# Packed attention and SwiGLU on one core: the sign of the float64 weights goes through a Prelu in the first pass of their conversion

## The chip, the cores and the metric

The kernel runs on one core of a Trainium2 chip. The metric is the device time of one execution in microseconds. A core has five engines with queues of their own: PE (TensorE, matrix products), DVE (VectorE), ACT (ScalarE), POOL (GpSimd) and SP (SyncE, which here issues the DMAs). Each takes the instructions of its queue in order and waits by semaphores for the others. All of them work on SBUF (128 partitions); products of PE land in PSUM.

## The reference

For 8 batches of 8 heads, 32 packed queries `p` attend to 576 keys and values, and then the 576 queries `q` attend to the 32 packed results. The heads are put side by side to 4608 tokens of 512 numbers, which pass an RMS norm and a SwiGLU layer:

```python
def _attn_ref(q, k, v, p):          # sm_attn: softmax attention, scale 1/sqrt(64)
    p_packed = sm_attn(p, k, v)
    out = sm_attn(q, p_packed, p_packed)
    return out.astype(np.float32)

def _moe_ref(x, w_gate, w_val, w_out, rms_g):
    rms = np.sqrt(np.mean(x * x, axis=-1, keepdims=True) + 1e-06)
    xn = x / rms * rms_g
    g = xn @ w_gate
    silu = g * (1.0 / (1.0 + np.exp(-g)))
    val = xn @ w_val
    return (silu * val @ w_out).astype(np.float32)
```

`q`, `k`, `v`, `p` and `rms_g` come as float32. The three weight matrices (512 x 1536, 512 x 1536, 1536 x 512) come as float64, and the kernel reads each number as two 32-bit words, a low one and a high one. The high word has the sign, 11 bits of exponent and the 20 upper bits of the mantissa.

## The kernel before, in words

The 4608 tokens are 12 units of 384 (`u`), a unit is 3 query tiles of 128 tokens. Products that have to be more exact than one half-precision product are made of three, with each operand split into a high and a low float16 part (`split`, L127: ACT writes the high part, L129, DVE the low part, L130).

The work before the steady loop is a prologue, whose order is written by hand in the string `PROLOGUE` (L24). Each letter advances a generator by one step: `s` is the packed attention of batch 0 (`stage1_gen`), `0 1 2` are the first three query tiles (`qtile_gen`), `u` the norm of unit 0 (`unit_gen`), `w` the weights (`weights_gen`), `p` the product of the packed results with the gate and value weights (`pw_gen`, `pw_chunk`, L471) and `a` the gate and value products of unit 0 (`moe_ft`, L667, with Silu in L674). After it, the loop over units runs 24 slots a unit, in which the next batches' attention and the next units' query tiles are laid between the products (`moe_ft`, then `moe_out` with the products `po`, L688). Tile's planner then puts the instructions of each engine into an order of its own by estimated costs, so that a queue's order is not everywhere that of the program.

`weights_gen` loads the weights in 18 chunks of 1 MB, each 128 partitions of 1024 float64 numbers. Chunks 1 to 12 are `w_gate` and `w_val` in turn (`load_gv`, two for each of six column blocks `c`), and the last six are `w_out` (`load_wo`). SP issues each load (L180, L206) into a raw buffer. The first twelve go round over five such buffers: three lie in the memory of `wo32`, which is not yet in use, and two are `wst` buffers; the last six share the two `wst` buffers. `to_f32` (L153) makes float32 of a chunk:

- L158: ACT reads the high words as if they were float32, takes the absolute value and multiplies by 2^-111 (`HI_SCALE`). The factor sets the exponent right for what follows.
- L159: DVE shifts the bits left by 3.
- L160: DVE ors the top three bits of the low words in.
- The sign, which Abs took away, is put back in one of two ways, by the letter in `SGW` (for the twelve) or `SGO` (for the six). With "D", DVE takes the sign bit of the high word and ors it in (L167). With "P", ACT writes the sign as 1 or -1 to a bfloat16 tile `sg` (L164), and POOL multiplies (L165). `sg` has the tag "o", of which there are two buffers; `sq` and later `o` use the same.

The letters alternate, so nine chunks have their sign put back by DVE and nine by ACT and POOL. After `to_f32` of a gate or value chunk, ACT squares the result to bfloat16 (`sq`, L187), PE sums the squares over the rows (L189), and DVE works out powers of two as scales from the largest sum (L194, `norm_scale`: L114, L118, L119, and L198); POOL multiplies them to `gv_sc` and `wo_sc` (L199 to L201). After a `w_out` chunk DVE takes the maxima (L211). When all six are there, `wo_scale` makes the scale (L218 to L227), and `wo_split` (L229) splits `w_out` in place, in six steps on ACT, DVE and POOL (L232 to L237); only then do the products `po` have their weights.

Between these, the prologue's query tiles run chains of small steps over PE, DVE, ACT and POOL: `rest_q` with the scores `ps` (L549), the maximum (L563), Exp (L566), the sum (L568), the reciprocal (L571), the normalisation (L572), the transposes (L610), the values `px` (L589) and their squares (L595), and POOL's norm (L597 to L602). `unit_gen` takes the norms of the three tiles together (L617, L619), and POOL multiplies the scales of the weights by the result (L658, L632).

Of the kernel before, what the change touches and what calls it, by code (L numbers as in the profile page):

```python
# [9 lines left out]
F32 = mybir.dt.float32  # L10
F16 = mybir.dt.float16
BF16 = mybir.dt.bfloat16
U32 = mybir.dt.uint32
AF = mybir.ActivationFunctionType
ALU = mybir.AluOpType
AX = mybir.AxisListType

P = 128
EXP_MASK = 0x7F800000

SGW = "PDPDPDPDPDPD"
SGO = "DPDPDP"
WOS = "ADADDA"
PROLOGUE = "s w " + "s " * 13 + "0 1 2 " * 5 + "u " * 4 + "w " * 18 + "p a a w " * 6 + "w " * 6  # L24

# [1 line left out]
HI_SCALE = 2.0**-111  # L27
# [3 lines left out]
def tile_packed_attention_then_swiglu(  # L31
# [27 lines left out]
    nc = tc.nc  # L59
# [17 lines left out]
    pool = ctx.enter_context(tc.tile_pool(name="pool", bufs=2))  # L77
# [22 lines left out]
    wo32 = cpool.tile([P, NFT, DM], F32, name="wo32")  # L100
# [11 lines left out]
    def norm_scale(u, s, sums):  # L112

        nc.vector.tensor_scalar(  # L114
            u.bitcast(U32), sums.bitcast(U32), 24, 23,
            ALU.logical_shift_right, ALU.logical_shift_left,
        )
        nc.vector.tensor_scalar(u, u, 2.0**-126, 2.0**51, ALU.max, ALU.mult)  # L118
        nc.vector.tensor_single_scalar(s.bitcast(U32), u.bitcast(U32), EXP_MASK, ALU.bitwise_xor)  # L119
# [30 lines left out]
    wctx = ExitStack()  # L150
    wpool = wctx.enter_context(tc.tile_pool(name="wpool", bufs=2))

    def to_f32(dst, st, pool_signs):  # L153


        lo, hi = st[..., 0], st[..., 1]
        d = dst.bitcast(U32)
        nc.scalar.activation(dst, hi.bitcast(F32), AF.Abs, scale=HI_SCALE)  # L158
        nc.vector.tensor_single_scalar(d, d, 3, ALU.logical_shift_left)  # L159
        nc.vector.scalar_tensor_tensor(d, lo, 29, d, ALU.logical_shift_right, ALU.bitwise_or)  # L160
        if pool_signs:
            sg = pool.tile([P, 1024], BF16, name="sg", tag="o", bufs=2)
            sg = sg.rearrange("p (a n) -> p a n", a=dst.shape[1])
            nc.scalar.activation(sg, hi.bitcast(F32), AF.Sign)  # L164
            nc.gpsimd.tensor_tensor(dst, dst, sg, ALU.mult)  # L165
        else:
            nc.vector.scalar_tensor_tensor(d, hi, 0x80000000, d, ALU.bitwise_and, ALU.bitwise_or)  # L167

    def load_gv(c):

        pn = ps_m.tile([P, 512], F32, name="pn", tag="pm")
        for n, w in enumerate((w_gate, w_val)):

            room = (2 * c + n) % 5
            if room < 3:
                raw = wo32[:, 4 * room : 4 * room + 4, :].bitcast(U32).rearrange("p a n -> p (a n)")
            else:
                raw = wpool.tile([P, 4 * DM], U32, name="wst", tag="wst", bufs=2)
            raw = raw.rearrange("p (k n e) -> p k n e", k=NKT, e=2)
            nc.sync.dma_start(  # L180
                raw.rearrange("p k n e -> p k (n e)"),
                w[:, 4 * c * P : 4 * (c + 1) * P].rearrange("(kt p) f -> p kt f", p=P),
            )
            x = wgv[:, c, :, n, :]
            to_f32(x, raw, SGW[2 * c + n] == "P")
            sq = pool.tile([P, NKT, 2 * P], BF16, name="sq", tag="o", bufs=2)
            nc.scalar.activation(sq, x, AF.Square)  # L187
            for kt in range(NKT):
                nc.tensor.matmul(  # L189
                    pn[:, 256 * n : 256 * n + 256], onesb, sq[:, kt, :], start=(kt == 0), stop=(kt == NKT - 1)  # L190
                )
            yield
        mx = wpool.tile([P, 2], F32, name="wmx", tag="w1", bufs=6)
        nc.vector.tensor_reduce(mx, pn.rearrange("p (w f) -> p w f", w=2), AX.X, ALU.max)  # L194
        u = wpool.tile([P, 2], F32, name="wu", tag="w1", bufs=6)
        s = wpool.tile([P, 2], F32, name="ws", tag="w1", bufs=6)
        norm_scale(u, s, mx)
        nc.vector.tensor_scalar_mul(pw_sc[:, c, :], s, 2.0**-15)  # L198
        nc.gpsimd.tensor_scalar(gv_sc[:, c, 0:1], u[:, 0:1], gmax, 2.0**-5, ALU.mult, ALU.mult)  # L199
        nc.gpsimd.tensor_scalar(gv_sc[:, c, 1:2], s[:, 0:1], gmax_r, 2.0**-12, ALU.mult, ALU.mult)  # L200
        nc.gpsimd.tensor_scalar(wo_sc[:, c : c + 1], u[:, 0:1], u[:, 1:2], gsq, ALU.mult, ALU.mult)  # L201

    def load_wo(i):

        raw = wpool.tile([P, 2, DM, 2], U32, name="wst", tag="wst", bufs=2)
        nc.sync.dma_start(  # L206
            raw.rearrange("p a n e -> p a (n e)"),
            w_out[2 * i * P : 2 * (i + 1) * P, :].rearrange("(a p) n -> p a n", p=P),
        )
        to_f32(wo32[:, 2 * i : 2 * i + 2, :], raw, SGO[i] == "P")  # L210
        nc.vector.tensor_reduce(  # L211
            wo_mx[:, 2 * i : 2 * i + 2], wo32[:, 2 * i : 2 * i + 2, :], AX.X, ALU.max, apply_absolute_value=True
        )
# [25 lines left out]
    def weights_gen():  # L239
        load_g()  # L240
        yield
        for c in range(NFC):
            yield from load_gv(c)
            yield
        for i in range(NFT // 2):
            load_wo(i)
            yield
        wo_scale()
        for i in range(NFT // 2):
            wo_split(i)  # L250
            yield
# [487 lines left out]
    for t in range(TPU, NU * TPU):  # L739
        u, i = divmod(t, TPU)  # L740
# [6 lines left out]
    for b in range(1, B):  # L747
        t = b * S // P
        u, i = divmod(t, TPU)
# [62 lines left out]
```

## Time and profile before

| | |
|---|---|
| median of three runs | 925.7 us (921.09 to 926.83) |
| the profiled execution | 921.36 us |
| its span | 919.6 us |
| mean granted clock of PE in it | 0.949 of full speed |
| busy PE, DVE, ACT, POOL | 771.5, 565.5, 563.8, 111.0 us |

The span is the time from the first to the last instruction in the profile; what is missing to the execution's own time (1.8 us) lies around it. Engines are busy side by side, so their busy times do not add up to the span. Busy shares over the whole span mix a prologue of some 170 us, in which PE is often idle, and the steady loop, in which PE is busy for most of the time. The chain of work that ended last starts at the last instruction and goes back, at each step to what released it, or to the instruction before it on its engine; it is given in order of time, as start, duration, engine, tile and line. A row of a line's instructions gives the minimum, median and maximum duration in ns. In a timeline, the bracket at the end says how long the engine was idle before the instruction and what released it.

### The profile page before, as it was taken

To read this page: it belongs to the slowest core of one execution; us is meant where nothing else is said; L and a number is where in the kernel's file an instruction comes from. 1 tells how busy PE (TensorE), PEld (TensorE's weight loads), DVE (VectorE), ACT (ScalarE), POOL (GpSimd) and SP (SyncE) were. 2 spreads that over 40 slices of the span, in tenths; PEclk is the share of its full clock that TensorE was granted. 3 is DMA by queue.
4 is the path that set the end of the run, shared out by engine and by line. 5 is a ranking of instruction groups with operands and counts; after the bars stand their busy time and mean duration, and the time that the engine had idled before them with its cause. 6 is when DMAs were issued, how large, how long until landed. Compare 5 with 4: busy or idle time off the path is not lost.

```text
span 919.6 us, 16693 instructions
## 1 busy us (share of the span) xinstructions
PE 771.5 (84%) x6392; PEld 435.4 (47%) x6392; DVE 565.5 (61%) x1406; ACT 563.8 (61%) x1074; POOL 111.0 (12%) x228
## 2 busy tenths in 40 slices
PE   4545866765889988898999988999999899989998
PEld 3332223324745544446745444557555345467453
DVE  4697796564755756846746657657647558466250
ACT  3465656545756758847756659657668479477240
POOL 2258111310000010010010000100000100100000
PEclk9856698996999999999999999999999999999999
DMA  9764327333083264224272282140751622221200
GB/s 248 252 201 146 100 84 153 83 81 64 7 181 92 52 145 93 43 58 81 56 178 64 52 195 55 39 100 7 139 132 32 135 53 53 58 65 24 57 1 35
DMA packets 174000, 84.98 MB, mean 92 GB/s; under 512 B 149216, under 2 KB 161504, under 8 KB 173920
## 3 DMA queue, kind: packets, MB, share of 16 engines
q1 hardware_dynamic: 173920, 83.91, 38.8%
q8 instruction: 50, 0.82, 0.4%
q14 instruction: 30, 0.25, 0.1%
HBM read 47.97 MB, written 9.44 MB: 62 GB/s over the span
## 4 chain that ended last, share of the span: by engine, by line
PE 41%; DVE 18%; ACT 17%; DMA 12%; issue 6%; POOL 3%; SPq 1%; ACTq 0%; DVEq 0%; POOLq 0%
PE po L688 14%; PE pg L667 8%; PE pv L667 7%; DMA aT<-ehl 5%; PE pp_w L471 4%; ACT t L674 3%; ACT L674 3%; PE px L589 2%; DVE t L675 2%; DVE pwt L130 2%; DMA kT<-khl 2%; DMA kf<-in_k_dram 2%; DVE h L678 1%; ACT pwt L129 1%; DMA aTu<-ahl 1%
## 5 line engine op out<-in xcount | busy, mean ns | idle before, releaser
L688 PE MATMUL po<-wo,h 128*128 128x512 f16 x1296 | 295.7, 383 | 3.8 <-ACT t L674 1.4
L667 PEld LDWEIGHTS <-pwt 128*128 128x128 f16 x2304 | 206.8, 99 | 155.5 <-issue 46.1
L667 PE MATMUL pg<-aTu,pwt 128*128 128x384 f16 (+1 forms) x1152 | 172.4, 292 | 42.0 <-ACT t L674 14.1
L688 PEld LDWEIGHTS <-h 128*128 128x128 f16 x1296 | 123.9, 99 | 156.5 <-issue 20.4
L667 PE MATMUL pv<-aTu,pwt 128*128 128x384 f16 (+1 forms) x1152 | 170.1, 291 | 2.6 <-DVE pwt L130 1.1
L675 DVE SCALAR_TENSOR_TENSOR t<-pv,usc,t 128x384 f32<-128x384 f32 x144 | 88.3, 614 | 49.5 <-PE pv L667 29.0
L130 DVE SCALAR_TENSOR_TENSOR pwt<-pp_w,pw_sc,pwt 128x256 f16<-128x256 f32 x192 | 84.1, 476 | 53.8 <-ACT pwt L129 52.2
L677 ACT CAST h<-t 128x384 f16<-128x384 f32 x144 | 73.1, 509 | 61.3 <-DVE t L675 61.0
L674 ACT ACTIVATE t<-pg,usc 128x384 f32<-128x384 f32 x144 | 83.1, 578 | 36.7 <-PE pg L667 35.7
L129 ACT ACTIVATE pwt<-pp_w,pw_sc 128x256 f16<-128x256 f32 x192 | 81.4, 471 | 27.9 <-PE pp_w L471 16.1
L678 DVE TENSOR_TENSOR h<-t,h 128x384 f16<-128x384 f32 x144 | 79.7, 555 | 22.5 <-ACT h L677 19.8
L595 ACT ACTIVATE px<-px 128x512 f32<-128x512 f32 x36 | 21.0, 584 | 85.7 <-PE px L589 85.6
L597 POOL TENSOR_SCALAR var<-ssx,eps 128x1 f32<-128x1 f32 x36 | 10.7, 298 | 421.4 <-ACT px L595 421.1
L471 PE MATMUL pp_w<-wgv,pg 64*32 64x512 f32 x768 | 59.1, 617 | 2.9 <-ACT t L674 2.1
L693 DVE TENSOR_SCALAR o<-po,invE 128x512 f32<-128x512 f32 x36 | 27.0, 749 | 50.1 <-PE po L688 38.6
L589 PE MATMUL px<-pav,aT 128*128 128x256 f16 (+1 forms) x240 | 32.9, 283 | 22.9 <-DMA aT<-ehl 22.9
L674 ACT ACT_TABLE_LOAD x35 | 44.9, 1283 | 1.4 <-PE pg L667 0.9
L563 DVE TENSOR_REDUCE mx<-ps 128x8 f32<-128x256 f32 x36 | 15.1, 420 | 40.6 <-PE ps L558 38.2
L566 ACT ACT_TABLE_LOAD x30 | 38.5, 1283 | 0.5
L589 PEld LDWEIGHTS <-aT 128*128 128x128 f16 (+1 forms) x240 | 20.7, 103 | 37.6 <-DMA aT<-ehl 34.5
L130 DVE SCALAR_TENSOR_TENSOR khl<-kf,sk,khl 96x768 f16<-96x768 f32 x28 | 27.8, 1009 | 0.5 <-ACT khl L129 0.5
L568 DVE TENSOR_REDUCE sm<-e 128x8 f32<-128x256 f32 x36 | 15.0, 417 | 19.3 <-ACT e L566 19.0
(267 smaller groups left out, 850.5 us busy)
## 6 DMA issues: line engine op xcount, KB each, us to landing
kf<-in_k_dram SPq DMA_DIRECT2D x16, 576.0 KB, 7.4
vf<-in_v_dram SPq DMA_DIRECT2D x16, 576.0 KB, 6.8
out_dram<-o SPq DMA_DIRECT2D x36, 256.0 KB, 2.2
qf<-in_q_dram SPq DMA_DIRECT2D x29, 256.0 KB, 3.4
wst<-in_moe_w_out_dram SPq DMA_DIRECT2D x6, 1024.0 KB, 5.0
wo<-in_moe_w_gate_dram SPq DMA_DIRECT2D x4, 1024.0 KB, 8.7
wo<-in_moe_w_val_dram SPq DMA_DIRECT2D x4, 1024.0 KB, 6.2
wst<-in_moe_w_val_dram SPq DMA_DIRECT2D x2, 1024.0 KB, 7.9
```

Of the source, the lines that this page charges most:

```text
L129: nc.scalar.activation(hi, x, AF.Copy, scale=s)
L130: nc.vector.scalar_tensor_tensor(lo, x, s, hi, ALU.mult, ALU.subtract)
L471: nc.tensor.matmul(ps[e][32 * j : 32 * j + 32, :], pg[h, j, :], wgv[h, c, j, :, :].rearrange("p w f -> p (w f)"), start=True, stop=True,)
L566: nc.scalar.activation(e, e, AF.Exp, scale=esc)
L589: nc.tensor.matmul(px[o : o + n, 256 * g : 256 * g + 256], aT[:, 2 * la + g, o : o + n], pav[g][:, lp, :], start=(j == 0), stop=(j == 2),)
L667: nc.tensor.matmul(ps[:, c0 : c0 + n], pw[:, g, lw, w, f * P : (f + 1) * P], aT[:, 2 * la + g, c0 : c0 + n], start=(j == 0), stop=(j == 5),)
L674: nc.scalar.activation(t, pss[0], AF.Silu, scale=sc[:, c, 0:1])
L675: nc.vector.scalar_tensor_tensor(t, pss[1], sc[:, c, 1:2], t, ALU.mult, ALU.mult)
L677: nc.scalar.copy(h[:, 0, :], t)
L678: nc.vector.tensor_tensor(h[:, 1, :], t, h[:, 0, :], ALU.subtract)
L688: nc.tensor.matmul(po, hs[ft][:, lh, ts], wo[:, ft, lw, :], start=(n == 0), stop=(n == 3 * NFT - 1))
L693: nc.vector.tensor_scalar_mul(o, po, invE)
```

## The change

In the first pass of `to_f32`, Abs is replaced by Prelu with a slope of -2^32: numbers below zero are multiplied by -2^32 after the scale. A negative number becomes positive by that, with an exponent field larger by 32. After the scale of 2^-111 the exponent fields of the weights are below 32, so this sets exactly one bit, bit 28, and the shift to the left by 3 moves it to bit 31, which is the sign. So the sign is in place after L159, and both ways of putting it back are gone, with the strings that chose between them. Nothing else is changed.

```diff
-SGW = "PDPDPDPDPDPD"
-SGO = "DPDPDP"
...
-    def to_f32(dst, st, pool_signs):
+    def to_f32(dst, st):
...
         lo, hi = st[..., 0], st[..., 1]
         d = dst.bitcast(U32)
-        nc.scalar.activation(dst, hi.bitcast(F32), AF.Abs, scale=HI_SCALE)
+        nc.scalar.activation(dst, hi.bitcast(F32), AF.Prelu, scale=HI_SCALE, alpha=-(2.0**32))
         nc.vector.tensor_single_scalar(d, d, 3, ALU.logical_shift_left)
         nc.vector.scalar_tensor_tensor(d, lo, 29, d, ALU.logical_shift_right, ALU.bitwise_or)
-        if pool_signs:
-            sg = pool.tile([P, 1024], BF16, name="sg", tag="o", bufs=2)
-            sg = sg.rearrange("p (a n) -> p a n", a=dst.shape[1])
-            nc.scalar.activation(sg, hi.bitcast(F32), AF.Sign)
-            nc.gpsimd.tensor_tensor(dst, dst, sg, ALU.mult)
-        else:
-            nc.vector.scalar_tensor_tensor(d, hi, 0x80000000, d, ALU.bitwise_and, ALU.bitwise_or)
...
-            to_f32(x, raw, SGW[2 * c + n] == "P")
+            to_f32(x, raw)
...
-        to_f32(wo32[:, 2 * i : 2 * i + 2, :], raw, SGO[i] == "P")
+        to_f32(wo32[:, 2 * i : 2 * i + 2, :], raw)
```

The line numbers of the prediction are those of the kernel before.

## The prediction

> **What bounds the kernel now.** I read the page first, then the table of stretches, the chain of work that ended last, and the timelines of VectorE (DVE), ScalarE (ACT) and GpSimd (POOL) between 0 and 180 us. The change touches only the conversion of the float64 weights, and by the rows of its lines all of that work lies between 15 and 137 us of a 919.6 us span. The table of stretches gives busy time by engine (PE, PE's weight loads, DVE, ACT, POOL), then the granted clock, the DMA share and GB/s:
>
> ```profile
> 40.00:60.00 20.00, 7.53 (x35) 6.15 (x36) 18.45 (x34) 13.50 (x17) 12.56 (x8) 0.61 0.59 181
> 60.00:80.00 20.00, 7.29 (x40) 4.86 (x39) 17.14 (x29) 12.41 (x18) 14.11 (x17) 0.67 0.67 224
> 80.00:100.00 20.00, 14.25 (x49) 4.20 (x47) 13.75 (x29) 11.61 (x18) 11.32 (x17) 0.53 0.17 34
> 100.00:120.00 20.00, 14.34 (x87) 6.08 (x86) 17.94 (x29) 13.37 (x24) 2.69 (x2) 0.83 0.43 150
> 120.00:140.00 20.00, 12.90 (x84) 5.36 (x83) 17.74 (x33) 10.38 (x21) 4.08 (x2) 0.91 0.16 53
> ...
> 200.00:220.00 20.00, 5.43 (x46) 4.02 (x45) 6.88 (x24) 7.58 (x17) 2.77 (x10) 0.62 0.23 51
> ```
>
> From 40 to 140 us DVE is busy for 17 to 18 of every 20 us, except between 80 and 100; PE and ACT have room. Before 36 us PE and the loads set the pace, and after about 150 us none of the changed lines runs. So what the change is worth is read from 40 to 140 us. These are the steps of the chain there (start, duration, engine, tile, line) that the change bears on, with two undisturbed ones (L572 at 56.97, L159 at 116.98) to compare with:
>
> ```profile
> 44.82 2.27 DVE e L572
> ...
> 52.44 1.39 DVE wu L114
> ...
> 55.85 1.12 DVE wgv L167
> 56.97 0.34 DVE e L572
> ...
> 62.90 1.96 DVE wu L114
> ...
> 70.28 2.12 POOL wgv L165
> ...
> 96.65 1.13 DVE wo L167
> ...
> 103.23 1.49 DVE up L123
> ...
> 116.98 0.57 DVE wo L159
> ...
> 120.02 1.81 DVE wo L159
> ...
> 134.37 2.33 POOL wo L165
> ```
>
> The reader is to see two things. The sign pass of DVE (L167) is itself on the chain, with 1.13 us each. And some tiny DVE instructions take far too long: L114 works on two columns and takes 1.39 and 1.96 us, L572 takes 2.27 in place of 0.34. The timelines of POOL and DVE show why:
>
> ```profile
> 62.72 2.12 POOL L165 TENSOR_TENSOR wgv<-wgv,sg 128x1024 f32<-128x1024 f32 x1 [4.09 <-DVE wgv L160]
> ...
> 81.02 2.12 POOL L165 TENSOR_TENSOR wgv<-wgv,sg 128x1024 f32<-128x1024 f32 x1
> 83.13 4.48 POOL L658 TENSOR_SCALAR usc<-gv_sc,uu 128x2 f32<-128x2 f32 x4
> ```
>
> ```profile
> 66.05 1.21 DVE L167 SCALAR_TENSOR_TENSOR wgv<-wo,wgv 128x1024 uint32<-128x1024 uint32 x1
> ...
> 75.14 0.15 DVE L114 TENSOR_SCALAR wu<-wmx 128x2 uint32<-128x2 uint32 x1
> ...
> 79.58 1.22 DVE L160 SCALAR_TENSOR_TENSOR wgv<-wo,wgv 128x1024 uint32<-128x1024 uint32 x1
> ...
> 81.53 2.70 DVE L160 SCALAR_TENSOR_TENSOR wgv<-wo,wgv 128x1024 uint32<-128x1024 uint32 x1
> ...
> 136.72 1.22 DVE L211 TENSOR_REDUCE wo_mx<-wo 128x2 f32<-128x1024 f32 x1 [1.23 <-POOL wo L165]
> ```
>
> POOL's pass from 62.72 ends at 64.84, and L114, begun at 62.90, ends at 64.86. POOL's pass from 81.02 ends at 83.14, and L160, begun at 81.53, ends at 84.23, which is 1.09 later, nearly its undisturbed 1.22. So the DVE instruction that meets POOL's sign pass stands still until that pass is over. A sign pass on POOL thus costs DVE up to 2 us as well.
>
> **What the change removes.** The rows of the three lines (minimum, median and maximum in ns, then first and last start):
>
> ```profile
> L167 DVE SCALAR_TENSOR_TENSOR wgv<-wo,wgv x4: 1209/1213/1226, 22.5 to 84.3; 128x1024 uint32<-128x1024 uint32 x4
> L167 DVE SCALAR_TENSOR_TENSOR wo<-wst,wo x3: 1210/1218/1222, 96.6 to 126.7; 128x1024 uint32<-128x1024 uint32 x3
> L167 DVE SCALAR_TENSOR_TENSOR wgv<-wst,wgv x2: 1207/1209/1211, 47.0 to 74.0; 128x1024 uint32<-128x1024 uint32 x2
> ...
> L164 ACT ACTIVATE sg<-wst x5: 1108/1113/1152, 50.4 to 128.5; 128x1024 bf16<-128x1024 f32 x5
> L164 ACT ACTIVATE sg<-wo x4: 1090/1100/1113, 16.0 to 76.6; 128x1024 bf16<-128x1024 f32 x4
> ...
> L165 POOL TENSOR_TENSOR wgv<-wgv,sg x6: 2118/2124/3085, 18.6 to 81.0; 128x1024 f32<-128x1024 f32 x6
> L165 POOL TENSOR_TENSOR wo<-wo,sg x3: 2133/2317/2319, 102.4 to 134.4; 128x1024 f32<-128x1024 f32 x3
> ```
>
> In engine time that is 9 x 1.21 = 10.9 us of DVE, 9 x 1.11 = 10 us of ACT, and 6 x 2.12 + 3 x 2.32 = 19.7 us of POOL, and with the last the stalls of DVE. What lies on the path, step by step, in order of time:
>
> - 44.82, the stall of L572 goes: 2.27 - 0.34 = 1.93. PE's transposes of that tile come next and start so much earlier.
> - 52.44, the stall of L114 goes: 1.39 less about 0.07 that an undisturbed one takes from the next start = 1.32. L167 at 55.85 goes: 1.12.
> - 62.90, the stall of L114 goes: 1.96 - 0.07 = 1.89. L167 at 66.05 goes: 1.13 from start to start (its neighbours on the chain show the same step).
> - 70.28, POOL's pass goes. What is late next is ACT: its L187 (next fence) waited 1.07 for this pass, and the activations of the query tiles that feed POOL's L597 stand behind it. I count 1.07, not 2.12.
> - 81.02, POOL's pass goes, and L658 behind it on POOL no longer waits until 83.13. Its input uu is written just before L160 starts at 81.53, so it can start at about 81.6: 1.5.
> - 96.65, L167 goes: 1.13.
> - 103.23, the stall of L123 goes: 1.49 - 0.07 = 1.42. 120.02, the stall of L159 goes: 1.81 - 0.57 = 1.24 by the chain.
> - 134.37, POOL's pass goes. L211 then waits for DVE's own work before it: 1.23.
>
> Sum: 1.93 + 1.32 + 1.12 + 1.89 + 1.13 + 1.07 + 1.5 + 1.13 + 1.42 + 1.24 + 1.23 = 15.0 us.
>
> Costed at nothing are the other L167 (22.5, 47.0, 74.0, 84.3, 111.4, 126.7). At 22.5 PE's transposes and scores cover them, at 47.0 and 111.4 DVE waits for PE or ACT right after, at 74.0 and 84.3 POOL's and PE's chain runs. Without those covers they are worth 6 x 1.13 = 6.8 us more. ACT's nine sign activations are costed at nothing because ACT is busy 10 to 14 of 20 us.
>
> **What the change adds and moves.** It adds no instruction; 18 activations (L158) change from Abs to Prelu with a slope.
>
> ```profile
> L158 ACT ACTIVATE wgv<-wo x8: 1117/1128/1145, 15.0 to 74.0; 128x1024 f32<-128x1024 f32 x8
> ```
>
> ```profile
> 72.43 1.06 ACT L187 ACTIVATE sq<-wgv 128x1024 bf16<-128x1024 f32 x1 [1.07 <-POOL wgv L165]
> ...
> 97.31 1.28 ACT L674 ACT_TABLE_LOAD   x1
> 98.60 0.58 ACT L674 ACTIVATE t<-pg,usc 128x384 f32<-128x384 f32 x1
> 99.08 1.47 ACT L398 ACTIVATE khl<-kf 96x1536 bf16<-96x1536 f32 x1
> ```
>
> Prelu is not in this trace. From below, it costs what Square (L187) does, 1.06 for the same number of elements, a gain of 18 x 0.07 = 1.3 us on ACT; from above, a table load of 1.28 us at every switch, priced among the rivals. I take 1.13 as before, since four functions over 1024 columns (Abs, Sign, Square, scaled Copy) all lie near 1.1. The Trainium skill, ScalarE: Activation LUTs, section What ACT_TABLE_LOAD costs, speaks a little against that: every operand that is a column pointer adds about 93 ns. If the slope were such a pointer, an estimate by that page is 18 x 0.093 = 1.7 us, and the sum would be 13.3 in place of 15.0; no row here shows an operand of that kind for Prelu.
>
> No DMA is moved. Each load's buffer is free after L160 now, not after L167 or L164, so SP's next load goes out up to 1.13 us earlier than the shift alone would give.
>
> ```profile
> SPq L180 <- DVE wgv L160: 24.1, 3, 16.5
> ```
>
> ```profile
> wo<-in_moe_w_gate_dram SPq DMA_DIRECT2D x4, 1024.0 KB, 8.7
> ```
>
> These are a row of SP's waits (total us, times, longest) and one of DMA issues. SP waits for buffers, not for the DMA engines, and a load lands 8.7 us after its issue. The wait is thus shortened with DVE's work; but if conversions outrun the loads, landing is late next. Five buffers at 8.7 us are one chunk each 1.7 us, while 12 chunks take DVE at least 2 x (0.6 + 1.13) = 3.5 us a pair: the loads keep up. Each sg also held one of the two buffers that sq uses; that goes too.
>
> **Time.** The profiled execution took 921.36 us, 4.3 under the median of the three runs (925.7). 921.4 - 15.0 = 906.4 against its own time, and the same gain off the median is 910.7. The time asked for is a median, so I take 910.
>
> **The rivals.**
>
> *The gain is mostly hidden.* PE takes its queue in order, at a granted clock of 0.53 to 0.67 between 40 and 100 us, and the scale of w_out waits behind the last matmuls of unit 0 whenever the maxima are ready. Then only the steps count that end in POOL's own pass or a stall in front of a PE step without another wait: 1.93 + 1.32 + 1.89 + 1.07 + 1.5 = 7.7 us, and 918. For it: PE is busy 14.3 us of 20 between 80 and 120. Against it: 17 to 18 of 20 for DVE.
>
> *More than the sum.* The six covered L167 count as well (6.8 us), and POOL's pass at 70.28 with its full 2.12 (1.05 more): 15.0 + 7.9 = 22.9, and 903. For it: once one cover shrinks, the pass under it would have come out. Against it: PE and ACT would have to shrink alike.
>
> *The order of the queues.* The instructions are not issued in the order of the program: L398 of batch 1, which the program reaches after the prologue, runs at 99.08, amid the weights. A planner sets the order, and with 27 instructions fewer it may set another, also behind 180 us, where the change does nothing. The stretch from 200 to 220 us has PE busy for only 5.43 us; if half of such a hole (7.3 us) came on top, the time would be 910 + 7 = 917; it could as well be taken away.
>
> *Table loads, on the slower side.* If Prelu is not in the table that holds Exp, nor in that of Silu, each switch costs a load, 1.28 us by the row at 97.31. By ACT's timeline the 18 L158 alternate with Exp and Silu such that 19 loads would be added: 19 x 1.28 = 24.3 us if all lie on the path, and 910 + 24 = 934. From 12 loads on the path upwards the gain is gone. Against it: Abs, Sign, Square, Copy and Exp run after one load until 97.31, and Abs and Sign also run between Silus without one. By the Trainium skill, ScalarE: Activation LUTs, section Table sets: the hidden batching unit, cheap functions are fillers of every set; it names relu and abs, not Prelu, and no run here shows it yet. The Trainium skill, on the same page, section What ACT_TABLE_LOAD costs, puts a switch at about 2.66 us with its drain, by which the estimate would be 50 us and 960; the row here shows 1.28 and the Silu directly behind it.
>
> **How the numbers follow.** The sum as it stands (gain of 10 to 18 us): 0.55. More than the sum: 0.13. Hidden: 0.20. Another order that eats half of the gain: 0.07. Table loads: 0.05. A measurement of this kernel tells about 1% from no change, which is 9.3 us, or 916.4. Faster by over 1% are the first two, 0.68; within 1% the hidden gain and the other order, 0.27; slower the table loads, 0.05. The likeliest case alone reaches from 905 to 916. To leave out no more than 2 in 10 the range goes up over the hidden gain and the other order to 921, which leaves the table loads out, and down to 900, a little under the 903 of the case with more.
>
> **What would show it.** Right: no DVE instruction between 36 and 140 us over 1.3 us; L572 and L114 always below 0.5; the wait of L187 for POOL gone, replaced by short ones for L160; PE's first matmul of po, now 15 us ahead of where the trace has it; everything after it as long as before. Wrong: new table loads; a Prelu of clearly over 1.13 us; the first matmul of po less than 9 us earlier, with PE or a load named by the waits that took over; or a po that is earlier and an end that is not, which would be the order of the queues.

## The result, and the profile after

The changed kernel takes 898.98 us (median of four runs, 898.36 to 899.42), the kernel before 924.09 us beside it (921.09 to 926.83): a ratio of 0.9728 with a 95% interval of 0.9693 to 0.9764, so 25 us less. The prediction was 910 us with a range from 900 to 921: the direction was right, the gain about 10 us too small, and the time lies 1 us outside the range. The two profiled executions stand at 921.36 and 899.14 us, 22.2 apart: that of the kernel before is 2.7 us under its median, and what the traces show is a gain of 22, not 25. All of that gain is made in the prologue, as these rows of the matmuls `po` show, of the kernel before and of the changed one (minimum, median and maximum in ns, first and last start):

```profile
L688 PE MATMUL po<-wo,h x1296: 375/379/635, 156.8 to 915.4; 128*128 128x512 f16 x186
```

```profile
L680 PE MATMUL po<-wo,h x1296: 376/379/634, 134.3 to 893.2; 128*128 128x512 f16 x186
```

The first `po` starts 22.5 us earlier and the last 22.2 us earlier: nothing is won or lost behind the prologue in these two executions. Where the other 3 us of the medians lie is not shown. The table of stretches of the changed kernel (busy us of PE, PE's weight loads, DVE, ACT, POOL; granted clock, DMA share, GB/s):

```profile
40.00:60.00 20.00, 10.10 (x45) 7.38 (x45) 17.94 (x42) 14.31 (x17) 8.89 (x9) 0.50 0.75 263
60.00:80.00 20.00, 11.10 (x59) 5.48 (x60) 11.64 (x26) 11.51 (x21) 10.16 (x23) 0.69 0.69 218
80.00:100.00 20.00, 13.73 (x92) 5.53 (x91) 19.68 (x38) 17.17 (x30) 2.67 (x4) 0.99 0.45 143
100.00:120.00 20.00, 15.93 (x112) 6.75 (x111) 18.45 (x41) 13.85 (x28) 0.00 (x0) 0.92 0.12 32
120.00:140.00 20.00, 12.62 (x120) 6.87 (x121) 9.76 (x27) 12.23 (x18) 4.71 (x3) 0.76 0.85 175
```

The stage that was at 100 to 140 us now lies between 80 and 120. DVE is still busy 18 to 20 of 20 us in it, but with the products of unit 0 and the other passes of w_out's conversion, and not with signs. The timeline of DVE in the changed kernel has the tiny instructions back at their size:

```profile
51.30 0.41 DVE L564 TENSOR_TENSOR e<-e,ri 128x256 f32<-128x256 f32 x1
...
60.91 0.16 DVE L112 TENSOR_SCALAR wu<-wmx 128x2 uint32<-128x2 uint32 x1
...
105.53 0.16 DVE L121 TENSOR_SCALAR up<-pm 128x2 uint32<-128x2 uint32 x1
```

These are the L572, L114 and L123 of the kernel before, which took up to 2.33, 2.05 and 1.56 us there when a sign pass of POOL ran. The rows of the first pass, now Prelu:

```profile
L157 ACT ACTIVATE wgv<-wo x8: 1107/1119/1134, 14.9 to 65.7; 128x1024 f32<-128x1024 f32 x8
L157 ACT ACTIVATE wo<-wst x6: 1117/1135/1148, 68.2 to 101.9; 128x1024 f32<-128x1024 f32 x6
L157 ACT ACTIVATE wgv<-wst x4: 1122/1128/1137, 38.4 to 58.5; 128x1024 f32<-128x1024 f32 x4
```

Prelu takes what Abs took. And its table is there: the chain of the changed kernel has the first load of Silu's table with a Prelu between the two Silus behind it.

```profile
82.60 1.28 ACT L666
83.89 0.58 ACT t L666
84.47 1.05 ACT wo L157
85.52 0.46 ACT t L666
85.98 0.40 ACT h L669
86.38 1.48 ACT khl L390 x2
```

These rows also show a new limit: between 82 and 90 us the chain runs along ACT, where in the kernel before, from 95.6 to 106.8 us, it had run along DVE.

When some steps start, in us of each profiled execution (the last four columns are experiments that are told below: nine DVE passes left; nine products on POOL added whose result goes aside, which means that hardly anything waits for it; both of these; ACT's signs and POOL's products left):

| | before | changed | DVE nine | aside | both | POOL half |
|---|---|---|---|---|---|---|
| maximum of the first query tile, DVE | 38.1 | 36.7 | 37.8 | 35.8 | 37.2 | 36.2 |
| sum of the tiles' norms (`pnu`), PE | 79.2 | 68.6 | 71.9 | 71.5 | 77.1 | 71.7 |
| scales `rr`, POOL | 87.6 | 74.2 | 76.8 | 78.8 | 86.3 | 79.3 |
| first Silu, ACT | 98.6 | 83.9 | 88.2 | 87.5 | 96.3 | 92.4 |
| last maxima of w_out, DVE | 136.7 | 108.8 | 118.8 | 114.4 | 129.6 | 126.0 |
| matmul of w_out's scale, PE | 148.8 | 126.2 | 127.5 | 133.0 | 139.6 | 141.5 |
| first `po`, PE | 156.8 | 134.3 | 135.2 | 141.0 | 146.7 | 149.5 |
| span | 919.6 | 897.3 | 898.3 | 903.1 | 912.1 | 913.1 |

### The profile page after: what moved, and what is told of

It reads as the page before. It is cut to its first block, busy times and chain, and to the rows that moved or that the text cites. A ratio compares the mean times of both kernels' runs of the same rounds, so it can differ in the third digit from the quotient of the medians.

```text
span 897.3 us, 16663 instructions
## 1 busy us (share of the span) xinstructions
PE 762.6 (85%) x6392; PEld 433.7 (48%) x6392; DVE 543.7 (61%) x1397; ACT 554.7 (62%) x1065; POOL 85.9 (10%) x219
## 4 chain that ended last, share of the span: by engine, by line
PE 41%; ACT 20%; DVE 16%; DMA 13%; issue 7%; POOL 2%; SPq 1%; ACTq 0%; DVEq 0%; POOLq 0%
PE po L680 13%; PE pg L659 8%; PE pv L659 8%; DMA aT<-ehl 6%; PE pp_w L463 4%; ACT t L666 3%; ACT L666 3%; PE px L581 2%; DMA kT<-khl 2%; DVE t L667 2%; DMA kf<-in_k_dram 2%; ACT pwt L127 2%; DVE pwt L128 1%; DMA aTu<-ahl 1%; ACT khl L390 1%
## 5 line engine op out<-in xcount | busy, mean ns | idle before, releaser
L659 PE MATMUL pg<-aTu,pwt 128*128 128x384 f16 (+1 forms) x1152 | 170.6, 289 | 38.7 <-ACT t L666 14.1
L659 PE MATMUL pv<-aTu,pwt 128*128 128x384 f16 (+1 forms) x1152 | 167.9, 289 | 1.3 <-DVE t L667 0.7
L587 ACT ACTIVATE px<-px 128x512 f32<-128x512 f32 x36 | 21.0, 584 | 87.6 <-PE px L581 87.4
L463 PE MATMUL pp_w<-wgv,pg 64*32 64x512 f32 x768 | 57.1, 613 | 2.9 <-ACT t L666 2.1
```

Source lines behind the costliest of these rows:

```text
L463: nc.tensor.matmul(ps[e][32 * j : 32 * j + 32, :], pg[h, j, :], wgv[h, c, j, :, :].rearrange("p w f -> p (w f)"), start=True, stop=True,)
L659: nc.tensor.matmul(ps[:, c0 : c0 + n], pw[:, g, lw, w, f * P : (f + 1) * P], aT[:, 2 * la + g, c0 : c0 + n], start=(j == 0), stop=(j == 5),)
```

## The experiments

All of them ask what the removed work was worth: the sum gave 15.0 us, 25 were measured. The theory of the prediction is that the sum's steps add, with six of the nine DVE passes and all sign activations of ACT at nothing. The rivals are that the covered passes count as well, that ACT counts, that the waits for POOL were sized too small, and that another order of the queues made the excess.

The runs were made in three groups, in which the kernel before had medians of 923.2, 921.7 and 922.3 us (924.1 beside the result), and the changed kernel ran only beside the result. A difference of medians out of two groups is therefore good to some 2 us: 0.5 cannot be told from 2.

**One half at a time.** Prelu in only nine of the 18 chunks, the other nine as before (X is Prelu, D is DVE's sign pass behind Abs, P is ACT's sign and POOL's product behind Abs):

```diff
-SGW = "PDPDPDPDPDPD"
-SGO = "DPDPDP"
+SGW = "XDXDXDXDXDXD"
+SGO = "DXDXDX"
```

> Prelu takes the sign along in the nine chunks whose sign ACT and POOL put back before; the other nine keep Abs and DVE's own sign pass. The sum of the prediction holds that this half is worth 1.93 + 1.32 + 1.89 + 1.07 + 1.5 + 1.42 + 1.24 + 1.23 = 11.6 us, so about 912.5 off the median of 924.1. The rival, that the covered passes count as well (each removed pass is worth its time from start to start, as the case of more than the sum has it), gives this half 12.7 us, 911.5: this run alone does not part the two, its complement does. A third theory, that another order of the queues brought the excess, expects the two halves not to add up to 25 us.

```diff
+SGW = "PXPXPXPXPXPX"
+SGO = "XPXPXP"
```

> The complement: Prelu takes the sign along in the nine chunks whose sign DVE put back before; the other nine keep Abs, ACT's sign and POOL's product. The sum of the prediction counts only three of the nine DVE passes, 3.4 us: about 920.7. If all nine count, 9 x 1.13 = 10.2 us: about 914. If order made the excess: anything, and the halves do not add.

The first took 901.05 us (ratio 0.9777, 0.9739 to 0.9815), the second 914.65 (0.9912, 0.9883 to 0.9941; its ten runs lie between 910.3 and 919.3), beside 923.21 for the kernel before. So taking away ACT's and POOL's half is worth 22 us and DVE's half 8.6: 31 together, where the whole change gives 25. They do not add. Read from the other end, nine DVE passes cost 2 us when POOL's and ACT's half is gone, and 8.6 us when it is there. Neither the sum (3.4 in any case) nor the rival that all nine always count (10.2) has that.

**Prelu itself.** Abs in its place, and no sign at all:

```diff
-        nc.scalar.activation(dst, hi.bitcast(F32), AF.Prelu, scale=HI_SCALE, alpha=-(2.0**32))
+        nc.scalar.activation(dst, hi.bitcast(F32), AF.Abs, scale=HI_SCALE)
```

> The changed kernel with Abs in place of Prelu: the sign is left out of the computation, and instructions and data flow are those of the changed kernel. If Prelu costs what Abs costs, 899 within 1 us. If the slope is a pointer operand of about 93 ns a time, up to 1.7 us less. If Prelu switches the table, far less.

900.03 us (0.9755, 0.9723 to 0.9787), with every queue in the same order as in the changed kernel. Prelu costs what Abs costs; the slope has no price that can be measured.

**All signs on DVE.**

```diff
+SGW = "DDDDDDDDDDDD"
+SGO = "DDDDDD"
```

> The kernel before with all 18 signs put back by DVE: no sign on ACT, no product on POOL, nine more DVE passes. If the stalls that POOL's pass causes and its own place on the path are worth 11.6 us and a DVE pass costs its 1.13 us only where it is on the path (3 of 9), about 924 - 11.6 + 3.4 = 916. If every DVE pass costs its 1.13 us, 924 - 12.7 + 10.2 = 921.5. Slower than 924 would say that POOL's half was not worth what I hold.

917.93 us (0.9956, 0.9931 to 0.9980), between the two expectations of 916 and 921.5, but for a reason that neither had. In the profiled execution, which took 923.29, 5 us over the median, the first `po` is at 144.1 us, 12.7 earlier than before; then all of that is lost. The chain of this kernel shows where:

```profile
159.69 9.13 DMA qf<-in_q_dram
...
171.88 4.01 DMA qT<-qhl
```

The load of the next query tile is on the chain with 9.13 us, at a place where the kernel before had work of ACT and DVE on it; SP's queue has another order here. The 24 matmul steps of unit 0 and the slots between (first to fourth `o` of a unit) take 101.9 us, 89.8 in the kernel before. I read this as the rival of the queues' order at work, in an experiment and not in the change; no run tried it. It says nothing on the price of a DVE pass, and I leave this run out of the sums.

**One cost at a time, put back into the changed kernel.** ACT's nine sign activations, with nobody who uses them:

```diff
+        if also:
+            nc.scalar.activation(hi.bitcast(F32), hi.bitcast(F32), AF.Sign)
```

> The changed kernel with ACT's nine sign activations put back, in the same nine chunks, written over the words that were read and used by nobody: ACT's 9 x 1.1 us alone, with no product on POOL. The prediction costed them at nothing: 899. The rival, that ACT is the next bound in the rounds with w_out (in the changed kernel it is busy 17.2 of 20 us there): up to 9 x 1.0 us more, 908.

POOL's nine products, aside, then in place:

```diff
+            nc.gpsimd.tensor_tensor(o4, x4, one4, ALU.mult)
```

> The changed kernel with nine products on POOL again (chunk times one), whose result goes aside in seven of nine (over memory that a later chunk fills), so that hardly anything waits for it: the stalls of DVE alone. By the sum 1.93 + 1.32 + 1.89 + 1.42 + 1.24 = 7.8 us more, 907. If the half of ACT and POOL is worth over 20 us because of the stalls, 9 x 1.7 = 15 us more, 914. If stalls are hidden, 899.

```diff
+            nc.gpsimd.tensor_tensor(x4, x4, one4, ALU.mult)
```

> As before, with the product written in place, so that squares and maxima wait for POOL as they did in the kernel before: stalls and place on the path. By the sum 11.6 us more, 910.5, and 3.8 more than with the product aside. If the waits for POOL are what the sum sized too small, the difference to the run before is 8 us or more.

The signs on ACT: 901.88 us (0.9779, 0.9743 to 0.9815), 2.9 more than the changed kernel (4.7 by the two ratios). The products aside: 905.10 (0.9817, 0.9777 to 0.9858), 6.1 more, where the sum's stalls gave 7.8; they cost DVE the stalls and POOL the time of the products, which nothing here parts. In place: 910.80 (0.9880, 0.9845 to 0.9915), 11.8 more, where the sum gave 11.6. The stalls come back with the products, as these rows of POOL and DVE in the kernel with products aside show:

```profile
53.89 2.13 POOL L164 TENSOR_TENSOR wgv<-wgv,onesb 128x1024 f32<-128x1024 f32 x1
```

```profile
54.10 1.94 DVE L112 TENSOR_SCALAR wu<-wmx 128x2 uint32<-128x2 uint32 x1
```

POOL's product ends at 56.02, the two-column instruction of DVE at 56.04. Nothing waits for that product, so the stall is not a matter of data. The Trainium skill, Advanced Engine Details and Errata, section GPSIMD Details, says that POOL shares a read and a write interface with DVE and conflicts with DVE instructions in a two-port performance mode or with two SBUF inputs. The trace does not name the mode of an instruction, but it agrees in that not every DVE instruction waits, as a later product of POOL in the same kernel and DVE beside it show:

```profile
71.40 2.12 POOL L164 TENSOR_TENSOR wgv<-wgv,onesb 128x1024 f32<-128x1024 f32 x1
```

```profile
71.70 0.16 DVE L616 TENSOR_REDUCE sums<-pnu 128x1 f32<-128x3 f32 x1 [1.59 <-PE pnu L614]
71.78 1.76 DVE L116 TENSOR_SCALAR wu<-wu 128x2 f32<-128x2 f32 x1
```

The reduction from PSUM takes its 0.16 us in the midst of the product, and the instruction behind it, from SBUF to SBUF, waits out the rest. So the prediction's sentence that a DVE instruction which meets POOL's pass stands still is too wide. In the kernel before, too, L568, a reduction within SBUF, took its 0.42 us at 52.02 beside the product from 51.67, and behind it L114 took 1.47.

**Is a DVE pass covered?** DVE's pass is put back into the nine other chunks of the two kernels with POOL's products:

```diff
+        else:
+            nc.vector.scalar_tensor_tensor(d, hi, 0x80000000, d, ALU.bitwise_and, ALU.bitwise_or)
```

> The product in place on POOL (times one) in nine chunks and DVE's sign pass in the other nine: the kernel before without ACT's sign activations. Added one at a time to the changed kernel, POOL's products in place cost 11.8 us and the DVE passes 2.1. If such costs add, 899 + 11.8 + 2.1 = 913. If a DVE pass is covered only as long as POOL does not stall DVE, the passes cost 8.6 us here, as they did beside ACT's sign and POOL's product: 919.5, and ACT's signs are the 3 to 4 us left to the kernel before.

> POOL's product aside (nothing waits for it in seven of nine) and DVE's sign pass in the other nine. If it is the stalls that use up the cover of the DVE passes, 899 + 6.1 + 8.6 = 913.7; if it is the waits of squares and maxima for POOL, 899 + 6.1 + 2.1 = 907.

With the products in place: 920.63 us (0.9975, 0.9952 to 0.9998), 9.8 more than without the passes. With the products aside: 912.75 (0.9887, 0.9853 to 0.9921), 7.7 more. Both are where the theory of a cover used up by POOL has them (919.5 and 913.7), and 6 to 8 us from where costs that add would be (913 and 907). That it happens with products for which hardly anything waits says that it does not need the waits of squares and maxima. What is left are the stalls of DVE and the time that the products take on POOL.

One pair of these kernels has the order of the queues nearly fixed. By their traces the kernel with nine DVE passes and the one with both have the same order of instructions on PE, ACT and POOL (POOL's products not counted), on DVE up to 118.8 us and on SP up to 123.7 us of the former. The products aside cost 11.7 us there (912.75 less 901.05). Without the passes they cost 6.1, between two kernels with one order on POOL and SP, and up to 69 us on PE, ACT and DVE. At the norms, where the order is still fixed within both pairs, the products have cost 5.2 us beside the passes and 2.9 without them.

The kernel with nine DVE passes and the products in place is the kernel before without ACT's signs; what is left to 922.32 us beside it is 1.7 us, hardly clear of nothing by its interval.

**A lucky order?** Nine DVE passes without POOL, in the other nine chunks than in the first experiment:

```diff
+SGW = "DXDXDXDXDXDX"
+SGO = "XDXDXD"
```

> Nine DVE sign passes and no POOL and no ACT sign, as in the first experiment, but in the other nine chunks. If nine passes are covered once POOL does not stall DVE, 901 again. If the 2 us of the first experiment were due to a lucky order of its queues, up to 9 x 1.13 = 10.2 us over 899, 909.

899.48 us (0.9745, 0.9712 to 0.9778): nine passes cost 0.5 us here and 2 in the first experiment. So the cover does not depend on which nine, as far as 2 us can be told.

**Two tries to win more.** In the changed kernel the last maxima of w_out start 28 us earlier than before, but the first `po` only 22.5 us. The matmul of the scale stands in PE's queue behind the last matmuls of unit 0, and its chain has a wait that is new there:

```profile
117.61 0.70 PE pp_w L463 x9
118.31 4.91 DMA kT<-khl
123.27 0.42 PE psc L331 x6
```

```diff
-PROLOGUE = "s w " + "s " * 13 + "0 1 2 " * 5 + "u " * 4 + "w " * 18 + "p a a w " * 6 + "w " * 6
+PROLOGUE = "s w " + "s " * 13 + "0 1 2 " * 5 + "u " * 4 + "w " * 18 + "p a a w w " * 6 + "w " * 6
```

> The changed kernel with the six w_out steps in the first three of the six rounds (two a round), and its scale and splits in the last three. In the changed kernel the maxima of w_out are ready at 110 us and the matmul of its scale runs at 126, behind the matmuls of unit 0, with 8 us more until the first po. If that tail is what the next step waits for, up to 8 us less, 891. If DVE's work in the rounds is the bound (19.7 and 18.5 of 20 us), it is only moved: 899.

```diff
+PROLOGUE = ... + "p a a w w " * 3 + "p a a " * 2 + "w " + "p a a " + "w " * 5
```

> The changed kernel with the six w_out steps in the first three rounds and only the scale and the first of its six splits ahead of the last round, the other splits behind it. If the wait of the scale's matmul behind unit 0 is worth something and the splits in the rounds were what made the version before slower, up to 8 us less, 891. If DVE and ACT in the rounds are the bound, 899 to 905.

The first took 904.47 us (0.9811, 0.9777 to 0.9844), slower than the changed kernel: its scale runs at 114.7, yet its first `po` at 140.6; ACT, DVE and POOL split w_out in the midst of the rounds there. The second took 899.28 (0.9753, 0.9724 to 0.9782): its first `po` is 2.7 us earlier, at 131.5, and its span 897.2, so the 2.7 us are given back within unit 0. Neither beats the changed kernel.

The medians in one view, by what stands beside Prelu or, in the last row, in its place (us):

| | without DVE's nine passes | with them |
|---|---|---|
| nothing | 899.0 | 901.1 and 899.5 |
| POOL's products, aside | 905.1 | 912.8 |
| POOL's products, in place | 910.8 | 920.6 |
| products in place and ACT's signs | 914.7 | 923.2 (before) |

## Why the prediction was too small

**POOL's half was sized right where it stands alone.** The steps at 44.82, 52.44, 62.90, 70.28, 81.02, 103.23, 120.02 and 134.37 sum to 11.6 us; put back alone, the products cost 11.8. But the steps were read in a kernel that has the DVE passes, and beside these the products cost 19.6 (920.63 less 901.05), so that the agreement is in part luck. Of the 11.6 the stalls were taken as 7.8; the products aside cost 6.1.

**ACT's nine sign activations were costed at nothing; that was wrong by some 2 to 4 us.** Put back alone they cost 2.9, and beside POOL's products 3.9 (914.7 less 910.8). The reason given, that ACT is busy for 10 to 14 of 20 us, is the share of busy time over a stretch, and in the changed kernel the chain runs along ACT between 82 and 90 us. Beside everything else the cost is not clear (1.7 us).

**The failed step is the one on the covers: "Costed at nothing are the other L167."** The sum counted three DVE passes, 3.4 us, and measured against the kernel before the nine are worth 8.6. Each cover was judged for itself, with all else in place: PE or ACT was late right behind a pass, so the pass was free. By the runs that lateness hangs on POOL's products: beside them nine passes cost 8.6, 9.8 and 7.7 us, without them 0.5 to 2, and the change takes both away. The books can be kept the other way round: then the passes are worth 2 us, where the sum had 3.4, and the products 19.6, where it had 11.6. Either way what is missing are the 6 to 8 us that the two cost together and neither costs alone. The prediction named the price (6.8 us more without the covers) and the case of more than the sum came out at 903, but with a chance of 0.13. It held that PE and ACT would have to shrink alike for a cover to end, and did not ask whether the half of ACT and POOL, which went in the same change, made it.

What the runs showed in its place: the passes and the products use up the same slack. Alone, nine passes cost 0.5 to 2 us and the products aside 6; together 14 (912.8 less 899.0). That the slack is one of DVE fits the stalls, but is argued and not shown. In the table of starts the excess grows along the prologue: the move that both make is larger than the two single moves together by 2.3 us at the norms, 4.5 at the first Silu and 4.8 at the first `po`.

One step between can be read off, the four small products `usc` on POOL (two columns each), on which the scales, the transposes and all of unit 0 wait. Their rows in the kernel before, then with both, then in the changed kernel:

```profile
L658 POOL TENSOR_SCALAR usc<-gv_sc,uu x5: 289/1277/1292, 83.1 to 89.3; 128x2 f32<-128x2 f32 x5
```

```profile
L660 POOL TENSOR_SCALAR usc<-gv_sc,uu x5: 284/1283/1410, 82.1 to 90.9; 128x2 f32<-128x2 f32 x5
```

```profile
L650 POOL TENSOR_SCALAR usc<-gv_sc,uu x6: 285/287/1277, 72.0 to 83.9; 128x2 f32<-128x2 f32 x6
```

And what DVE does meanwhile, in the kernel before and in the kernel with both:

```profile
84.28 1.21 DVE L167 SCALAR_TENSOR_TENSOR wgv<-wo,wgv 128x1024 uint32<-128x1024 uint32 x1
...
86.23 1.23 DVE L160 SCALAR_TENSOR_TENSOR wo<-wst,wo 128x1024 uint32<-128x1024 uint32 x1
```

```profile
82.23 1.21 DVE L169 SCALAR_TENSOR_TENSOR wgv<-wo,wgv 128x1024 uint32<-128x1024 uint32 x1
83.36 0.15 DVE L112 TENSOR_SCALAR wu<-wmx 128x2 uint32<-128x2 uint32 x1
83.44 1.21 DVE L162 SCALAR_TENSOR_TENSOR wo<-wst,wo 128x1024 uint32<-128x1024 uint32 x1
84.57 0.15 DVE L116 TENSOR_SCALAR wu<-wu 128x2 f32<-128x2 f32 x1
84.68 1.23 DVE L169 SCALAR_TENSOR_TENSOR wo<-wst,wo 128x1024 uint32<-128x1024 uint32 x1
```

A two-column product of POOL takes 0.29 us, but 1.28 where DVE passes of 1.2 us (L169 is the sign pass here, L162 a conversion) follow one on another. So a pass of DVE delays POOL's small steps, as POOL's product delays DVE's. The sum had read this step as 1.5 us for the start of `usc` alone and took its 4.48 us for four as given; in the changed kernel five take 2.25. That is a size that the sum missed. But it is not the excess, since it comes with the DVE passes alone as well, in part one step later, as these rows of that kernel show:

```profile
74.47 2.39 POOL L660 TENSOR_SCALAR usc<-gv_sc,uu 128x2 f32<-128x2 f32 x4
76.83 2.40 POOL L634 TENSOR_TENSOR rr<-ru,su 128x1 f32<-128x1 f32 x3
```

From the start of `usc` to the end of `rr` it takes 4.8 us, the kernel with both 4.6, the changed kernel and the one with products aside 2.7. At the end of `rr` the moves fail to add by 2.9 us. Which steps make the excess, before the norms and behind `rr`, stays open.

**The rivals.** Table loads did not come: the page of either kernel counts 35 loads ahead of Silu and 30 ahead of the query tiles' Exp. The order of the queues did change, but only among the instructions of the prologue; from the first `po` to the end of the span both kernels take 763 us. How much of the prologue's gain is due to its order is not shown. Against a large part stand the pair with nearly one order, in which the products cost 11.7 us, and the last three sums of costs, which came within 2 us (919.5, 913.7 and 901 expected; 920.6, 912.8 and 899.5 measured). The hidden gain did not come: the first `po` is 22.5 us earlier, so PE's waits did not hide the change.

A rival that no run holds fixed is the granted clock of PE. Between 80 and 95 us it was 0.50 in the kernel before and 1.00 in the changed one; with both it was 0.50 from 80 to 90. The first products `pg` took 0.48 to 0.53 us each before and 0.32 to 0.34 in the changed kernel. Between the scales and the first Silu, where PE is on the chain of the kernel before with 6.4 us and of the changed kernel with 3.2, a part of the excess can be the clock's.

**The range.** It ended at 900, 3 us under the case with more. With ACT's 2 to 4 us taken off that case's 903 as well, the low end would have been 899 to 901, about where the time came out.

## What to carry to other kernels

Two costs that are each hidden by the other's lateness are not free: when a change takes both away, count both, and test a cover by asking whether what makes it is itself part of what goes. Where DVE and POOL run passes of a microsecond side by side, look for tiny instructions on either engine that take as long as the other's pass: moving work from DVE to POOL can then cost DVE as well. The busy share of an engine does not say what a pass on it is worth: nine passes of DVE, which was busy 17 to 18 of 20 us, were worth 8.6 us beside POOL's products and 0.5 to 2 without them.

## What the hardware showed that was not expected

The blocking between DVE and POOL goes both ways. DVE's two-column instruction waited up to 1.9 us for a product of 2.1 us on POOL, and POOL's two-column product, 0.29 us long, took 1.28 beside DVE passes of 1.2 us. The prediction had only the first of the two. And it is not every instruction: what waited on DVE beside POOL's product in the rows above works within SBUF (L112, L114, L116), while reductions took their own 0.16 and 0.42 us there. On POOL's side, too, four `usc` in the kernel with products aside took 0.28 us each beside a reduction of DVE of 1.22 us, L208 at 77.67. Prelu with a slope takes 1.12 to 1.14 us for 128 x 1024 numbers, as Abs does, and needs no table beside those of Exp and Silu.
